# A chunked delta-rule recurrence with a gated output layer: the loads of SP put into the planned order, output stores of one batch row each, and the range flag computed inside the main path

## The chip, the cores and the metric

The kernel runs on one core of a Trainium2 chip. A core has five engines with a queue each: PE (TensorE, the matrix products), DVE (VectorE), ACT (ScalarE), POOL (GpSimd) and SP (SyncE, which here only issues DMAs). DMAs are issued from SP, ACT and POOL and move data between HBM and the on-chip SBUF. Every queue is worked off strictly in its order; an instruction that has to wait holds up all that stand behind it on its engine. The metric is the device time of one execution in microseconds. Three executions of the kernel before took 483.6 us in the median (479.5 to 491.18).

## The reference

For 4 batches and 8 heads a state of 40x40 is carried over 768 steps, read out before each update; the readings of all heads make a sequence of 320 channels, which goes through a causal convolution of 5 taps with a sigmoid (the gate), a product with `w_val`, and a product with `w_out`:

```python
for t in range(S):                                  # S = 768, state (4, 8, 40, 40) starts at 0
    y[:, :, t] = einsum('bhd,bhde->bhe', rt, state)
    Sa = einsum('bhde,bhe->bhd', state, at)
    state = state * wt[:, :, None, :] - einsum('bhd,bhe->bhde', Sa, bt) + einsum('bhd,bhe->bhde', vt, kt)
x = y.transpose(0, 2, 1, 3).reshape(B, S, 320)
gate = 1 / (1 + exp(-sum_k conv_w[k] * x_shifted[k]))   # 5 taps, causal
out = (gate * (x @ w_val)) @ w_out                      # float32, (4, 768, 320)
```

## The kernel before

The 768 steps are cut into 12 chunks of 64 (`C = 64`), and within a chunk the recurrence is written as matrix products. The 32 sequences (4 batches, 8 heads) lie as 16 pairs in two halves of the partitions. The work on a chunk `c` is made of these steps, which are the functions inside `fast_path`:

- `load`, `load2`, `load3`: SP loads of the chunk's inputs: `w` (the decays, 520 KB), `kb` (keys and b, 1 MB), `a` (512 KB), `vp` (320 KB), `vt` (1 MB) and `ra` (832 KB).
- `prep`: two scans on DVE over the decays (L409, L412), then the scaled `a`, `b` and `k` (L418, L420). On ACT, `far` and `out_of` (L416, L417) turn the decays into a measure, `wmx`, of whether any is outside the range for which the chunked form is exact; they overwrite the buffer of the decays, so the next decays can be loaded into it only after them. PE then makes a block product (`mb_`, L426), whose result ACT copies out in four pieces (`lst`, L430 and L433, and `mb`, L434).
- `ak` (PE L444, then DVE L446) and `turn` (transposes on PE L456, copied by ACT L458).
- `tri`: the inverse of 32x32 triangles for two chunks at once on DVE, a chain of short steps (L467, L488, L490, L494). `solve` puts the 64x64 inverse together from it (PE L513, L530, L538 with copies on ACT L534, L536 and L545).
- `chain`: the part that carries the state from chunk to chunk, in two halves (PE L561, L559, L570, L577, L587, L603, L601, L619), with copies on ACT and DVE between the products. Its output is `xe` (DVE L614).
- `moe`: `xd` moves `xe` into the channel layout `xt` by 12 small DMAs inside SBUF (8 for the first half of the heads, 4 for the second), issued from POOL (L664). The convolution starts on ACT (L669) and goes on with 12 steps on DVE (L673), the sigmoid is ACT L677, the first product PE L83 in two parts with DVE L679 and L682 behind them, the second product PE L106. ACT L686 copies the result out and ACT L688 stores it, two batches (160 KB) per DMA, so two stores a chunk.

`weigh` unpacks the weights at the start: five loads and 40 short DVE instructions (L45 to L52).

The order of all this is not written by hand: `Plan` holds each step with its engine, an assumed duration and what it reads and writes, lays out the steps by a list scheduler, and emits them in the order of the planned start. PE, ACT, DVE and POOL keep that order (`manual_schedule`, L732). SP is not in that list: its loads are in the plan, but their order on the queue is set by the framework's own scheduler afterwards. Which buffer of a ring a load goes to, and so what it waits for, is the same in both cases.

After the main path, `general_path` computes a flag from `wmx` (L747 to L753: a maximum on DVE, a transposition on PE, a second maximum and a comparison on DVE), every engine loads it into a register (L754) and branches (L755) past a step-by-step version of the whole computation, which runs only if a decay was out of range. The tiles of that path lie in memory that the main path used, so the flag's own tiles wait until the main path, its stores included, is done with it.

```python
    with tc.manual_schedule(engines={E.PE, E.Activation, E.DVE, E.Pool}):       # L732
        for t, e, d, n, fn in seq:
            fn()
```

## Time and profile before

| | |
|---|---|
| runs | 479.5, 483.6, 491.18 us; median 483.6 |
| profiled execution | 486.17 us, of which the span from the first to the last instruction is 484.3 |
| PE busy | 381.4 us (79%) |
| DVE busy | 361.0 us (75%) |
| ACT busy | 222.7 us (46%) |
| POOL busy | 80.6 us (17%) |
| PE clock granted, mean | 0.904 of full speed |
| chain that ended last | PE 52%, DVE 19%, DMA 11%, waiting for nothing that shows 8%, ACT 6% |

The share of an engine is a mean over stages with different limits, so it does not say what a stage is worth. The first 30 us are filled by loads (the DMA engines are busy at 0.9 and more, then fall off), from there to about 100 us DVE is nearly always busy, from 100 to 450 us PE and DVE share the load, and the last 35 us belong to the output layer of the last two chunks and to the end of the program. All times below are on the span's own clock, 0 being its first instruction.

### The profile page before, as it was taken

The numbers are of one execution on the slowest core, as the hardware profiler recorded it, in microseconds if no ns is written. First come the engines' busy times: TensorE is split into PE (matmuls) and PEld (weight loads), VectorE is DVE, ScalarE is ACT, GpSimd is POOL, SyncE is SP. The second block draws the span as 40 slices with busy tenths as digits, with TensorE's granted clock in tenths as the row PEclk, the third lists the DMA queues.
The fourth block names the chain that finished last, engine by engine and source line by source line (L and its number), as shares of the span: only waits on it lengthen the run. The fifth ranks groups of instructions, "written<-read, shape, count | busy, mean of one in ns | idle before, by whom it ended". The sixth has DMA issues, their size and how long they took to land.

```text
span 484.3 us, 19768 instructions
## 1 busy us (share of the span) xinstructions
PE 381.4 (79%) x8857; PEld 328.6 (68%) x8857; DVE 361.0 (75%) x743; ACT 222.7 (46%) x393; POOL 80.6 (17%) x193
## 2 busy tenths in 40 slices
PE   0337566979989899779699789899897996989850
PEld 0226456969868797668588577897777975879630
DVE  8747787997888999869869959999888863314510
ACT  3443446445576362664264475446754263133210
POOL 2000000040310311301300400405005031050500
PEclk9999575897999999989979979999998997988995
DMA  8943333045534537151646322565106052010110
GB/s 342 420 166 133 115 104 94 23 177 194 193 106 138 188 110 294 42 172 50 205 167 206 117 74 90 207 204 181 60 18 208 24 182 62 7 49 10 30 35 23
DMA packets 19048, 63.20 MB, mean 130 GB/s; under 512 B 4080, under 2 KB 8168, under 8 KB 15888
## 3 DMA queue, kind: packets, MB, share of 16 engines
q1 hardware_dynamic: 11232, 53.78, 31.4%
q0 software_dynamic: 4608, 4.19, 3.4%
q10 hardware_dynamic: 3120, 3.93, 2.5%
q8 instruction: 70, 1.15, 1.0%
q14 instruction: 18, 0.15, 0.1%
HBM read 53.77 MB, written 3.93 MB: 119 GB/s over the span
## 4 chain that ended last, share of the span: by engine, by line
PE 52%; DVE 19%; DMA 11%; issue 8%; ACT 6%; POOL 1%; SPq 1%; ACTq 0%; DVEq 0%; POOLq 0%
PE pm L83 8%; PE pc L587 6%; PE pc L601 5%; PE pp L456 5%; PE pp L444 4%; DMA xt<-xe 4%; DVE x L490 4%; DVE tm L488 3%; PE pm L106 3%; PE pc L577 3%; DMA w<-in_w 3%; PE pc L570 3%; PE pc L603 3%; DVE mu L589 2%; DVE ag L673 2%
## 5 line engine op out<-in xcount | busy, mean ns | idle before, releaser
L664 POOL DMA_DIRECT2D xt<-xe x144 | 72.9, 514 | 240.9 <-issue 84.3
L673 DVE SCALAR_TENSOR_TENSOR ag<-xt,wts,ag 128x256 f32<-128x256 f32 (+1 forms) x144 | 55.7, 433 | 42.4 <-ACT ag L669 42.1
L490 DVE TENSOR_TENSOR x<-x,tm 128x58 f32<-128x58 f32 (+9 forms) x164 | 52.1, 318 | 3.1
L488 DVE TENSOR_TENSOR tm<-x 128x58 f32<-128x58 f32 (+9 forms) x164 | 52.1, 318 | 3.0
L83 PE MATMUL pm<-xt,wts 128*128 128x128 f32 (+1 forms) x288 | 39.9, 304 | 11.3 <-issue 4.7
L587 PE MATMUL pc<-ra,vu 64*128 64x64 f32 x768 | 47.4, 273 | 0.0
L587 PEld LDWEIGHTS pc<-ra,vu 64*128 64x128 f32 x768 | 45.0, 188 | 2.1 <-issue 0.3
L83 PEld LDWEIGHTS pm<-xt,wts 128*128 128x128 f32 (+1 forms) x288 | 31.8, 188 | 16.3 <-issue 5.7
L601 PE MATMUL pc<-mu,kbt 128*64 128x104 f32 x768 | 39.8, 256 | 2.2 <-issue 2.2
L106 PE MATMUL pm<-wts,ag 128*128 128x320 f32 (+1 forms) x144 | 37.7, 456 | 1.6 <-DVE ag L682 1.6
L444 PE MATMUL pp<-at,kb 64*64 64x64 f32 x768 | 31.0, 248 | 10.0 <-ACT mb L434 8.2
L601 PEld LDWEIGHTS pc<-mu,kbt 128*64 128x64 f32 x768 | 34.8, 137 | 5.5 <-issue 2.3
L444 PEld LDWEIGHTS pp<-at,kb 64*64 64x64 f32 x768 | 29.4, 162 | 12.1 <-ACT mb L434 9.1
L456 PE MATMUL pp<-cst,kb 104*128 104x104 f32 x192 | 28.2, 303 | 11.6 <-DVE ak L446 9.9
L426 PE MATMUL pp<-at,kb 64*64 64x64 f32 x768 | 18.6, 259 | 21.4 <-DVE at L418 15.4
L561 PE MATMUL pc<-vp,ak 64*64 64x40 f32 x768 | 29.9, 252 | 3.8 <-issue 3.8
L456 PEld LDWEIGHTS pp<-cst,kb 104*128 104x128 f32 x192 | 22.9, 170 | 14.2 <-DVE ak L446 11.2
L426 PEld LDWEIGHTS pp<-at,kb 64*64 64x64 f32 x768 | 16.6, 170 | 22.8 <-DVE at L418 15.4
L409 DVE TENSOR_TENSOR_SCAN lam<-w,ind 104x1040 f32<-104x1040 f32 x11 | 25.4, 2308 | 9.0 <-DMA w<-in_w 9.0
L589 DVE TENSOR_TENSOR mu<-pc,cst 128x1024 f32<-128x1024 f32 x24 | 29.2, 1216 | 3.2 <-PE pc L587 3.1
L458 ACT COPY kbt<-pp 128x640 f32<-128x640 f32 x24 | 16.6, 691 | 31.6 <-PE pp L456 21.5
L559 PE MATMUL pc<-st,at 64*64 64x40 f32 x704 | 27.7, 247 | 3.9 <-issue 3.9
(104 smaller groups left out, 704.7 us busy)
## 6 DMA issues: line engine op xcount, KB each, us to landing
kb<-in_kb SPq DMA_DIRECT2D x12, 1024.0 KB
vu<-in_vt SPq DMA_DIRECT2D x12, 1024.0 KB
ra<-in_ra SPq DMA_DIRECT2D x12, 832.0 KB
at<-in_a SPq DMA_DIRECT2D x12, 512.0 KB
w<-in_w SPq DMA_DIRECT2D x11, 520.0 KB
vp<-in_vp SPq DMA_DIRECT2D x12, 320.0 KB
out<-xt ACTq DMA_DIRECT2D x24, 160.0 KB
xt<-xe POOLq DMA_DIRECT2D x72, 42.5 KB, 3.4
```

Of the source, the lines that this page charges most:

```text
L83: T.matmul(out=o, lhsT=wv[k][r, m * 128:min(m * 128 + 128, DM)], rhs=rhs, start=(k == 0), stop=(k == 2))
L106: nc.tensor.matmul(out=ps[:, j, 0:DM], lhsT=gv[r, q * C:q * C + 128], rhs=wo[k][r], start=(k == 0), stop=(k == 2))
L426: T.matmul(out=PP[rows(par ^ s, 64), s, q * C:q * C + C], lhsT=KB[kb][rk, 2 * q + s, 1], rhs=at[rk, 2 * q + s], start=True, stop=True)
L444: T.matmul(out=PP[r, s, q * C:q * C + C], lhsT=KB[kb][r, 2 * q + s, 0], rhs=AT[n][r, 2 * q + s], start=True, stop=True)
L456: T.transpose(out=PP[:, i // 4, i % 4 * 128:i % 4 * 128 + ER], in_=KB[kb][0:ER, 8 * x + i].rearrange("p b t -> p (b t)"), identity=ident[0 ...
L488: V.tensor_tensor(out=tv, in0=part(32 * (j + 1) + j, *b, (32, n), (0, j)), in1=part(32 * j, *b, (0, n), (1, j)), op=ALU.mult)
L490: V.tensor_tensor(out=x, in0=x, in1=tv, op=ALU.subtract)
L587: T.matmul(out=ps[:, s, i * C:i * C + C], lhsT=vu[r, 8 * hf + i].rearrange("p b t -> p (b t)"), rhs=ra[r, w, 0:C], start=True, stop=True)
L589: op(("ge", c, hf), "DVE", dve(1024), lambda: V.tensor_tensor(out=mu[:, :, 0:C].rearrange("p (i s) t -> p s i t", s=2), in0=ps.rearrange(" ...
L601: T.matmul(out=o, lhsT=KBT[k][:, y * D:y * D + C], rhs=mu[:, 2 * (4 * p + q4) + s], start=(not c and not q4), stop=(q4 == 3))
L664: G.dma_start(out=o, in_=x)
L673: op(("cv", c, j, k), "DVE", 90 + 1.05 * nn[k], lambda k=k, q=q, j=j: V.scalar_tensor_tensor(out=acc[:, q], in0=xt[:, q, j:j + C], scalar= ...
```

## The change

- SP joins the engines whose order is the plan's (`manual_schedule`).
- Each store is one batch row: four DMAs of 64 rows of 1280 bytes (80 KB) a chunk, all on ACT, except in the last chunk, where two of the four are on SP.
- The 12 small moves of `xd` of the last two chunks are issued from SP instead of POOL.
- The flag is computed by four steps of the plan (`beyond`) while the main path is still at work, in a tile that the main path's memory does not hold.
- The loop of the step-by-step path goes over 16 steps instead of 32, 48 times instead of 24, and its output product and store are cut to match; this path does not run here.

Since the plan is made anew with these durations, the order on all engines moves, not only on SP.

```diff
-CG = 32
+CG = 16
...
+    def beyond():
+
+        wm, w1 = new("wm", [ER, 1]), new("w1", [1, 1])
+        op("wm", "DVE", 200, lambda: V.tensor_reduce(out=wm, in_=wmx.rearrange("p c x -> p (c x)"), axis=AX.X, op=ALU.max), r=[("wmx", c) for c in range(nch)], w=["wm"])
+        op("wt", "PE", 350, lambda: T.transpose(out=PP[0:1, 0, 0:ER], in_=wm, identity=ident[0:ER, 0:ER]), r=["wm", "cst"], w=ppb[0:1])
+        op("w1", "DVE", 250, lambda: V.tensor_reduce(out=w1, in_=PP[0:1, 0, 0:ER], axis=AX.X, op=ALU.max), r=ppb[0:1], w=["w1"])
+        op("fl", "DVE", 150, lambda: V.tensor_scalar(out=fl, in0=w1, scalar1=0.0, scalar2=None, op0=ALU.is_gt), r=["w1"], w=["fl"])
...
         for hf in range(2):
+            late = c + 2 >= nch
+
             def xd(hf=hf):
                 for o, x in x_moves(xt, XE[i], C, hf):
-                    G.dma_start(out=o, in_=x)
-            op(("xd", c, hf), "POOL", (8, 4)[hf] * 600, xd, r=[("xe", i, hf), ("xe", i, "c"), "wts"], w=[("xt", i), ("os", i)], lat=2500)
+                    (nc.sync if late else G).dma_start(out=o, in_=x)
+            op(("xd", c, hf), "SP" if late else "POOL", (8, 4)[hf] * (400 if late else 600), xd, r=[("xe", i, hf), ("xe", i, "c"), "wts"], w=[("xt", i), ("os", i)], lat=2500)
...
-        for j in range(2):
-            op(("store", c, j), "ACT", 560, lambda j=j: A.dma_start(out=out[j * 2:(j + 1) * 2, c * C:c * C + C], in_=os[:, j * DM:j * DM + DM]), r=[("os", i)], lat=2500)
+        for b in range(B):
+            on, eng = ("SP", nc.sync) if c + 1 == nch and b % 2 else ("ACT", A)
+            op(("store", c, b), on, 560, lambda b=b, eng=eng: eng.dma_start(
+                out=out[b, c * C:c * C + C], in_=os[b % 2 * 64:b % 2 * 64 + 64, b // 2 * DM:b // 2 * DM + DM]), r=[("os", i)], lat=2000)
...
+        if c + 4 == nch:
+            beyond()
...
-    with tc.manual_schedule(engines={E.PE, E.Activation, E.DVE, E.Pool}):
+    with tc.manual_schedule(engines={E.PE, E.Activation, E.DVE, E.Pool, E.SP}):
...
-        wm = cp.tile([ER, 1], F32, name="wm")
-        V.tensor_reduce(out=wm, in_=wmx.rearrange("p c x -> p (c x)"), axis=AX.X, op=ALU.max)
-        ps = pp.tile([1, ER], F32, name="pg")
-        T.transpose(out=ps, in_=wm, identity=cst[0:ER, 0:ER])
-        w1 = cp.tile([1, 1], F32, name="w1")
-        V.tensor_reduce(out=w1, in_=ps, axis=AX.X, op=ALU.max)
-        fl = cp.tile([1, 1], I32, name="fl")
-        V.tensor_scalar(out=fl, in0=w1, scalar1=0.0, scalar2=None, op0=ALU.is_gt)
         flag = nc.values_load(fl, min_val=0, max_val=1)
```

Three places of the new order. The first is SP's queue at the start of the program, from its eighth load on (`ag` and `xt` take the packed weights here, `at` is `a`; the line numbers of the changed kernel are higher by one). Before:

```order
L330 DMA ag<-in_wts 128x646
L330 DMA at_73<-in_a 128x1024
L330 DMA at_74<-in_a 128x1024
L330 DMA xt<-in_wts 128x646
L330 DMA vp<-in_vp 128x640
L330 DMA vu_81<-in_vt 128x2048
L330 DMA ra_83<-in_ra 128x1664
L330 DMA vu_82<-in_vt 128x2048
L330 DMA ra_84<-in_ra 128x1664
L330 DMA w<-in_w 128x1040
```

Now:

```order
L331 DMA ag<-in_wts 128x646
L331 DMA w<-in_w 128x1040
L331 DMA at_74<-in_a 128x1024
L331 DMA at_75<-in_a 128x1024
L331 DMA xt<-in_wts 128x646
L331 DMA vp<-in_vp 128x640
```

The decays of chunk 2 have moved ahead of eight other loads, from the seventeenth place to the ninth.

The second is ACT's queue in the same stretch (`xe` holds the decays of chunk 1 here, so its two lines are `far` and `out_of` of that chunk; `lst` and `mb` are the copies of the block product of chunk 0, then of chunk 1). Before:

```order
L430 COPY lst<-pp 128x16x32
L433 COPY lst<-pp 32x16x32 x2
L434 COPY mb<-pp 128x512
L520 ACTIVATE n_92<-lst,cst 128x16x16 x2
L430 COPY lst<-pp 128x16x32
L433 COPY lst<-pp 32x16x32 x2
L434 COPY mb<-pp 128x512
L416 ACTIVATE xe_108<-xe_108,bias 104x16x64
L417 ACTIVATE xe_108,wmx<-xe_108,bias 104x16x64
```

Now:

```order
L431 COPY lst<-pp 128x16x32
L434 COPY lst<-pp 32x16x32
L417 ACTIVATE xe_109<-xe_109,bias 104x16x64
L434 COPY lst<-pp 32x16x32
L418 ACTIVATE xe_109,wmx<-xe_109,bias 104x16x64
L435 COPY mb<-pp 128x512
L529 ACTIVATE n_93<-lst,cst 128x16x16 x2
L431 COPY lst<-pp 128x16x32
L434 COPY lst<-pp 32x16x32 x2
L435 COPY mb<-pp 128x512
```

The two range instructions of chunk 1 stood behind the copies of both block products and now stand ahead of the last copies of the first.

The third is the end of the program on PE and ACT, from the last chunk's `chain` on (PE: L577 and L587 are its middle, L603 and L601 its end, L83 the first and L106 the second product of the output layer, first of chunk 10, then of chunk 11). PE before:

```order
L577 MATMUL pc_114<-cst,vu_82 128x104 x8
L587 MATMUL pc_113<-ra_84,vu_82 128x64 x16
L587 MATMUL pc_114<-ra_84,vu_82 128x64 x16
L603 MATMUL pc_113<-ra_84,zd 64x104 x16
L601 MATMUL pc_113<-mu_103,kbt_90 64x104 x16
L603 MATMUL pc_114<-ra_84,zd 64x104 x16
L601 MATMUL pc_114<-mu_104,kbt_90 64x104 x16
L83 MATMUL pm<-xt,wts 128x128 x4
L83 MATMUL pm<-xt,wz 128x128 x2
L83 MATMUL pm<-xt,wts 128x128 x4
L83 MATMUL pm<-xt,wz 128x128 x2
L83 MATMUL pm<-xt,wts 64x128 x4
```

PE now:

```order
L83 MATMUL pm<-xt,wts 128x128 x4
L83 MATMUL pm<-xt,wz 128x128 x2
L83 MATMUL pm<-xt,wts 128x128 x4
L83 MATMUL pm<-xt,wz 128x128 x2
L586 MATMUL pc_115<-cst,vu_83 128x104 x8
L596 MATMUL pc_114<-ra_85,vu_83 128x64 x16
L596 MATMUL pc_115<-ra_85,vu_83 128x64 x16
L612 MATMUL pc_114<-ra_85,zd 64x104 x16
L610 MATMUL pc_114<-mu_104,kbt_91 64x104 x16
L612 MATMUL pc_115<-ra_85,zd 64x104 x16
L610 MATMUL pc_115<-mu_105,kbt_91 64x104 x16
L83 MATMUL pm<-xt,wts 64x128 x4
```

ACT before, from the sigmoid of chunk 10 on:

```order
L677 ACTIVATE ag<-ag 128x640
L669 ACTIVATE ag<-xt,wts 128x256 x2
L669 ACTIVATE ag<-xt,wts 128x128
L686 COPY xt<-pm 128x640
L688 DMA out<-xt 2x64x320 x2
L677 ACTIVATE ag<-ag 128x640
L686 COPY xt<-pm 128x640
L688 DMA out<-xt 2x64x320 x2
L754 TENSOR_LOAD fl
```

ACT now:

```order
L688 ACTIVATE ag<-ag 128x640
L588 COPY mu_105<-pc_115 128x16x40
L697 COPY xt<-pm 128x640
L680 ACTIVATE ag<-xt,wts 128x256 x2
L680 ACTIVATE ag<-xt,wts 128x128
L700 DMA out<-xt 64x320 x4
L688 ACTIVATE ag<-ag 128x640
L697 COPY xt<-pm 128x640
L700 DMA out<-xt 64x320 x2
L761 TENSOR_LOAD fl
```

The larger part of chunk 10's first product has moved from behind the last `chain` into it, and the copy of chunk 10's result (L697, before L686) from behind the start of chunk 11's convolution to ahead of it.

## Rows read from the trace of the kernel before

**Rows 1.** The chain of waits, end of the program: start us, length us, what.

```profile
464.29 3.18 PE pm L106 x12
...
467.50 0.70 ACT xt L686
...
468.78 8.55 DMA out<-xt
...
477.65 0.18 DVE wm L747
...
478.57 0.14 DVE fl L753
```

**Rows 2.** Busy time by stretch (engines, granted PE clock, DMA share, GB/s).

```profile
473.70:477.00 3.30, 0.00 (x0) 0.00 (x0) 0.00 (x0) 0.00 (x0) 0.00 (x0) 0.50 0.13 48
5.00:16.00 11.00, 0.64 (x24) 0.65 (x28) 10.87 (x10) 2.39 (x3) 0.00 (x0) 1.00 1.01 412
```

**Rows 3.** Lines L754, L755, L870: count, ns min/median/max, first and last start.

```profile
L754 PEldq TENSOR_LOAD <-fl x1: 493/493/493, 478.9 to 478.9; - x1
...
L755 SPq EVENT_SEMAPHORE  x8: 17/17/17, 479.9 to 480.4; - x8
L755 SPq COMPARE_BRANCH  x1: 45/45/45, 479.4 to 479.4; - x1
...
L755 PEldq EVENT_SEMAPHORE  x1: 51/51/51, 483.3 to 483.3; - x1
...
L870 SPq EVENT_SEMAPHORE  x10: 17/28/2212, 480.8 to 484.3; - x10
```

**Rows 4.** Groups by form: count, busy us, mean ns, idle before and its releaser.

```profile
L409 DVE TENSOR_TENSOR_SCAN lam<-w,ind 104x1040 f32<-104x1040 f32 x11 | 25.4, 2308 | 9.0 <-DMA w<-in_w 9.0
...
L418 DVE TENSOR_TENSOR at<-at,lam 104x1024 f32<-104x1024 f32 x12 | 14.3, 1192 | 0.0
```

**Rows 5.** The chain of waits at the head, columns as in rows 1.

```profile
4.75 11.23 DMA at<-in_a
16.07 13.78 DMA w<-in_w
```

**Rows 6.** Timeline of the head: start, length, engine, line, what, idle before, releaser.

```profile
24.36 2.02 ACT L433 COPY lst<-pp 32x512 f32<-32x512 f32 x2
...
26.88 1.15 ACT L416 ACTIVATE xe<-xe,bias 104x1024 f32<-104x1024 f32 x1
...
27.04 3.68 PE L444 MATMUL pp<-at,kb 64*64 64x64 f32 x64 [3.79 <-ACT mb L434]
...
29.97 2.33 DVE L409 TENSOR_TENSOR_SCAN lam<-w,ind 104x1040 f32<-104x1040 f32 x1 [9.02 <-DMA w<-in_w]
...
36.39 1.22 DVE L446 TENSOR_TENSOR ak<-pp,cst 128x1024 f32<-128x1024 f32 x1
```

**Rows 7.** Issues of the stores; ACT's waits by line (total us, times, longest).

```profile
L688 ACTq DMA_DIRECT2D out<-xt x24: 521/527/1122, 144.2 to 468.8; - x24
...
ACT xx L534 <- PE pm L530: 19.7, 9, 4.9
```

**Rows 8.** Tile xt, 440 to 460 us: the small moves, and issue to landing.

```profile
L664 POOL DMA_DIRECT2D xt<-xe x12: 502/512/522, 449.3 to 454.8; - x12
...
DMA to landing us min/median/max: 1.6/1.7/1.8
```

**Rows 9.** The chain of waits: the first products of chunks 9 and 10.

```profile
405.27 5.85 PE pm L83 x24
...
449.67 3.04 PE pm L83 x24
```

**Rows 10.** Timeline of chunk 11's convolution, columns as in rows 6.

```profile
456.73 0.80 ACT L669 ACTIVATE ag<-xt,wts 128x256 f32<-128x256 f32 x2 [0.99 <-DMA xt<-xe]
...
461.21 0.74 ACT L677 ACTIVATE ag<-ag 128x640 f32<-128x640 f32 x1 [2.35 <-DVE ag L673]
```

**Rows 11.** Busy time by stretch, columns as in rows 2: chunk 9's first product.

```profile
405.20:411.20 6.00, 5.93 (x25) 4.80 (x26) 4.39 (x12) 2.17 (x5) 0.00 (x0) 0.50 0.01 5
```

More of the change, by code (lines that the diff above doesn't have):

```diff
@@ L96, in out_mms @@
             q = 8 * L if k == 2 else (4 * k + 2 * h) * L
-            nc.tensor.matmul(out=ps[r], lhsT=gv[rk, q:q + 64], rhs=wo[k][rk], start=(k == 0), stop=(k == 2))
+            nc.tensor.matmul(out=ps[h * 64:h * 64 + 2 * L], lhsT=gv[rk, q:q + 2 * L], rhs=wo[k][rk], start=(k == 0), stop=(k == 2))
 def out_mms2(nc, ps, gv, wo):
@@ L135, in moe_steps @@
     os_ = mo.tile([128, DM], F32, name="os", bufs=1)
-    A.copy(out=os_, in_=ps[:, 0:DM])
-    for b in range(B):
-        store(b, os_[b * L:b * L + L])
+    for h in (0, 64):
+        A.copy(out=os_[h:h + 2 * L], in_=ps[h:h + 2 * L, 0:DM])
+        for j in range(2):
+            store(h // 32 + j, os_[h + j * L:h + j * L + L])
 class Plan:
@@ L271, in act, with fast_path @@
     return 165 + 0.84 * n
-def fast_path(ctx, tc, ins, out, nch, cst, wts, wz, wmx):
+def fast_path(ctx, tc, ins, out, nch, cst, wts, wz, wmx, fl):
     nc = tc.nc
@@ L416, in prep @@
         op(("far", c), "ACT", act(1024) + 100, lambda: A.activation(out=wv, in_=wv, func=AF.Abs, bias=bias[:, 0:1]), r=["bias"], w=wk)
-        op(("out_of", c), "ACT", act(1024) + 290, lambda: A.activation(out=wv, in_=wv, func=AF.Relu, bias=bias[:, 1:2], accum_out=wmx[:, c]), r=["bias"], w=wk)
+        op(("out_of", c), "ACT", act(1024) + 290, lambda: A.activation(out=wv, in_=wv, func=AF.Relu, bias=bias[:, 1:2], accum_out=wmx[:, c]), r=["bias"], w=wk + [("wmx", c)])
         op(("at", c), "DVE", 65 + 1.05 * 1024, lambda: V.tensor_tensor(out=at[0:ER], in0=at[0:ER], in1=lam[:, :, 0:C], op=ALU.mult), r=[("lam", n)], w=[("at", n)])
@@ L731, in fast_path, with general_path @@
     seq = plan.order()
-    with tc.manual_schedule(engines={E.PE, E.Activation, E.DVE, E.Pool}):
+    with tc.manual_schedule(engines={E.PE, E.Activation, E.DVE, E.Pool, E.SP}):
         for t, e, d, n, fn in seq:
             fn()
-def general_path(tc, ins, out, nch, cst, wts, wz, wmx):
+def general_path(tc, ins, out, nch, cst, wts, wz, fl):
     nc = tc.nc
@@ L793, in general_path @@
                     V.tensor_tensor(out=s, in0=s, in1=t2, op=ALU.add)
[L794 removed]
+                V.tensor_copy(out=xe[:, :, 0:4], in_=xe[:, :, CG:CG + 4])
                 for par in range(2):
                     r = slice(par * 64, par * 64 + 40)
[L797 removed]
+                    V.tensor_copy(out=xe[r, :, 4:CG + 4], in_=py[r].rearrange("p t u -> p u t"))
                 moe_steps(nc, mo, pp, wts, wz, xe, xt, lambda b, o: nc.sync.dma_start(out=out[b, bass.ds(c * CG, CG)], in_=o))
@@ L807, in rwkv_kernel @@
         wmx = keep.tile([ER, nch, 1], F32, name="wmx")
+        fl = keep.tile([1, 1], I32, name="fl")
         with ExitStack() as ctx:
-            fast_path(ctx, tc, ins, out, nch, cst, wts, wz, wmx)
-        general_path(tc, ins, out, S // CG, cst, wts, wz, wmx)
+            fast_path(ctx, tc, ins, out, nch, cst, wts, wz, wmx, fl)
+        general_path(tc, ins, out, S // CG, cst, wts, wz, fl)
 def lay_out(r, k, v, w, a, b, moe_w_val, moe_conv_w, moe_w_out):
```

2 lines of the change are left out of this document (removed).

## The prediction

> **What bounds the kernel now.** The chain of waits comes first, read from its end. ACT's last copy is over at 468.20; after it nothing is computed but the flag. The second store of the last chunk is issued at 468.78 and lands at 477.33, the flag's steps take 1.1 us from 477.65 to 478.71, and the span ends at 484.3 [rows 1]: 16.1 us behind the last useful instruction. Busy time by stretch says why the landing is late: while the two stores are all that moves, the DMA engines are busy at 0.13, two of sixteen, and move 48 GB/s; the first loads, spread over 128 partitions, keep all busy (1.01) at 412 GB/s [rows 2]. The lines of the branch show what follows the flag: PE loads its register at 478.9 and is past the branch at 483.3, 4.4 us later, and 1.0 us after that the span ends. SP goes from its branch at 479.4 over eight semaphore resets (0.07 apart) to its final waits at 480.8 [rows 3]. None of this is work, and all of it stands in a row, because the flag waited for the stores and the branch for the flag.
>
> At the other end of the program the groups by form show that, of all scans of the decays, those of L409 lost 9.0 us to a load [rows 4]. The chain at the head shows which load: that of chunk 2's decays, issued at 16.07 and landed at 29.85 [rows 5]. DVE stood still for 9.02 us ahead of 29.97, that is from 20.95 on [rows 6]. Between the two ends PE and DVE share the time and no load is waited for at this scale, so there only the new order can cost or give something.
>
> **The end of the program.** From 468.20 on, ACT issues its two stores of the last chunk and SP its two at the same time; an issue takes 0.53 [rows 7], so the last ones start at 468.78, as before. The landing of a store of one batch is in no row. The near end: the small moves inside SBUF land 1.6 to 1.8 us after their issue when nothing else is in flight [rows 8]. The far end: 8.55 us, as now [rows 1]. I take 2.0. A batch row has 64 outer rows, like the loads' 128 partitions and unlike the two batches of the present store, so I expect all sixteen engines, and then 80 KB at 412 GB/s are 0.2 us on top of 1.8. That is 470.8. SP then needs the 1.4 us from its branch to its final waits and about 0.4 for six more of those at 0.07 [rows 3], and the program 1.0 to end: 473.6. PE isn't later: it waits for no store any more, its last product ends at 467.47 [rows 1], and 4.4 us for register and branch make 471.9, under the store's shadow. Against 484.3 that is **-10.7**. The flag itself leaves the end. Ends of this term: -12 (landing after 1.6, part of the resets done ahead of it), and -4.2 with the far landing (477.33 + 1.8 + 1.0 = 480.1).
>
> The Trainium skill, DMA: Bandwidth & Descriptors, section "Why a DMA increments its semaphore by 16 and not by 1", says that a DMA runs on the largest number of engines up to 16 that divides the slowest dimension above 1 of both sides: two for the store of two batches, which the trace bears out (0.13 of the engines), and sixteen for one batch, which no row here shows. The same page's "Rules for kernel authors" speaks against the change: merge small transfers, since under 64 KB overhead is most of them. With its fit of 2.0 us plus 436 GB/s, a store of 160 KB would be an estimated 2.4 us and one of 80 KB 2.2, so splitting would give 0.2 and the sum would keep the rest only if the stores were not slow now. The trace disagrees, with 8.55 us.
>
> **The head.** Chunk 2's decays become SP's ninth load. Their buffer is free once chunk 0's two range instructions are through, which head ACT's queue in both orders. The load that is ninth now, of the same size, lands at 15.98 [rows 5]. So these land at about 16, before DVE wants them, and the 9.02 us go. What is late next: DVE's queue now holds, between 20.95 and the first triangle, the scan, a second one of the same length (2.31), a scaling (1.19) and a few short steps that I put at 1 us, some 6.8 to 27.7 [rows 4]. The triangle needs ACT's copies of chunk 1's block product, which ended at 26.38 [rows 6]. But the two range instructions of chunk 1, 1.15 each, which stood behind them, now stand ahead of chunk 0's last copies, so all copies behind are 2.3 later: 28.7 for the triangle, and the PE product, begun at 27.04, ends at 27.04 + 2.3 + 3.68 = 33.0. DVE's masking, next in its queue, starts then instead of at 36.39. New idle: 1.0 ahead of the triangle, and, its transposition (1.2, as the masking) done at 29.9, about 3.1 between it and the masking. Of 9.02 remain 4.9 on DVE, 3.4 on PE's side. But by the first inverse the new queue has three times the weight unpacking behind it, 21 of the 40 steps instead of 7, and the first inverse is what the chain of chunk 0 waits for. So I take **-2**; ends: 0 (all spent on moved work) and -9.
>
> **The last two chunks.** Before, chunk 10's first product (3.04 and a smaller rest) ran wholly behind the last chain [rows 9]; now the larger part is ahead of its middle. That shortens what comes behind and lengthens the chain by up to 3.04. Chunk 11's layer cannot use the gain: its convolution needs the moved `xe`, the last of which arrives at 456.73 in the present trace [rows 10], 7.1 after the chain's end at 449.67, and ACT's sigmoid at 461.21 waits for that convolution. ACT's new order puts chunk 10's copy ahead of the convolution, where ACT waits for the moves anyway. So the time from the chain's end to the end of ACT's last copy (468.20 - 449.67 = 18.5) stays, but PE now has little to do in the first 7.1 us of it. What such a gap costs is seen in chunk 9: after its wait for the moves the first product took 5.85 at a granted clock of 0.50 (1.2 instead of 2.4 GHz), not 3.04 [rows 9, 11]. Here the smaller rest and the 3.18 of the last product would follow, which at half the clock and double the time is up to about 4 more. With 0 to 3.0 for the chain and 0 to 4 for the clock I take **+2**, near the lower end, since the chain has gaps to fill.
>
> **Costed at nothing.** Two more store issues on ACT in each of eleven chunks: next on ACT come copies that wait for PE anyway (19.7 us in nine waits, 2.2 each, against 1.1) [rows 7]. Without that cover it is 22 x 0.53 = 11.6. The flag's four steps, 1.1 us [rows 1], stand beside DVE's wait for chunk 10's moves; bare they are 1.1. The 24 moves on SP: an SP issue is in no row that shows its length; ACT's of 0.53 and POOL's of 0.51 are the nearest [rows 7, 8], so I take the moves to be issued no later. Their landing from SP is in no row; 1 us either way is the bound, worth as much at the end. Behind them on SP stand only the flag's register and two stores. The general path doesn't run.
>
> **Sum.** -10.7 - 2 + 2 = -10.7 against the profiled execution's 486.2 (484.3 of span and 1.9 around it): 475.5. The median of the runs is 2.6 lower, so 472.9, said as **473**.
>
> **Rivals.** (a) *The head's gain holds*: DVE is nearly always busy from 30 to 100 us, so that idle time taken out there may carry through; against it, ACT's new order makes PE wait. With -9 for -2 and nothing lost at the end: 464. (b) *The end of chunk 11 eats more*: clock and chain at their bounds, +7, and nothing from the head: 480. (c) *A store of one batch lands no sooner* (on few engines, or because four share them): -4.2 for -10.7 is 479.5; the loads' row speaks against it. (d) *Slower*: ACT's added issues are not covered. The place is behind each chunk's output copy, ahead of the copies that `solve` and `chain` wait for; it decides as soon as ACT reaches those copies later than PE has their input, that is when the 2.2 us of mean wait shrink below 1.1. Then +11.6 stand against -10.7, and with (b)'s +7 it is 491. (e) *The loads move but nothing waits less*: the decays' place is seen in the order, so only the 2 us of the head are at stake: 475.
>
> **Numbers.** About 2% is what a measurement of this kernel can tell from no change, that is 473.9 or less for faster and 493.3 or more for slower. The forecast has 0.56 (467 to 479; some three fifths of it under 473.9), (a) 0.16, (b) 0.13, (c) 0.05, (d) 0.06, (e) 0.04. That makes 0.52 faster, 0.45 within 2%, 0.03 slower. The range runs from (a) to short of (d): 463 to 484.
>
> **What would show it.** Right: the last landing about 2 us after its issue, a DMA share near 1 for a moment, and less than 6 us from ACT's last copy to the end; no wait of L410 for a load; DVE's first masking near 33. Wrong: more than 8 us behind the last copy (first step); a wait of DVE for a load anywhere, or the first chain's output no earlier than before (second); a time from the last chain to the last copy far from 18.5 (third); ACT's copies behind the stores waited for by PE (rival d).

## The result, and the profile after

The changed kernel takes 468.47 us in the median of 4 runs (466.9 to 470.34), the kernel before 483.99 beside it; the ratio is 0.9711 (0.9631 to 0.9791), so it is faster. The forecast was 473, with a range from 463 to 484. The profiled execution took 468.85, with a span of 467.1, against 486.17 and 484.3. Some executions of a kernel come out a few per cent slower than its others: the ratios here and below leave out those more than 1.5% above the fastest, the medians do not.

The number came out near, but not by the sum that gave it. The span falls into four stretches; the bounds are the end of chunk 0's and of chunk 11's chain (the last `xe` of each, DVE) and the end of ACT's last copy (the prediction's 18.5 from the last chain to the last copy begins 0.7 earlier, at PE's end of that chain):

| profiled execution, us | before | changed | difference | forecast |
|---|---|---|---|---|
| start to the end of chunk 0's chain | 104.8 | 113.2 | +8.4 | -2 for all up to the last chains |
| from there to the end of chunk 11's chain | 345.6 | 325.6 | -20.0 | not in the sum |
| last chain to ACT's last copy | 17.8 | 21.7 | +3.9 | +2 |
| last copy to the end | 16.1 | 6.6 | -9.5 | -10.7 |

**The end.** The chain of waits of the changed kernel, its last part (start, length, what), now stops at ACT's last copy; no wait for a store or a flag stands in it [rows 1]:

```profile
453.49 1.05 PE pm L83 x12
...
454.90 4.85 PE pm L106 x12
...
459.82 0.69 ACT xt L697
```

The line of the branch, L762 (count, ns, first and last start) [rows 3]:

```profile
L762 SPq EVENT_SEMAPHORE  x8: 17/17/17, 464.8 to 465.4; - x8
...
L762 PEldq COMPARE_BRANCH  x1: 375/375/375, 455.6 to 455.6; - x1
...
L762 PEldq EVENT_SEMAPHORE  x1: 51/51/51, 459.8 to 459.8; - x1
L762 SPq COMPARE_BRANCH  x1: 45/45/45, 462.0 to 462.0; - x1
```

PE's queue takes the branch at 455.6, while its last products still run, and is through at 459.8, under ACT's last copy. Busy time by stretch shows the four row stores (columns as in rows 2; the DMA share is the last but one):

```profile
461.70:463.20 1.50, 0.00 (x0) 0.00 (x0) 0.00 (x0) 0.00 (x0) 0.00 (x0) 0.71 0.82 224
```

The four move at 0.82 of the engines and 224 GB/s, where two stores of two batches had 0.13 and 48. What is new at the end is on SP: it branches at 462.0 and does its first reset only at 464.8, 2.8 us later, where it took 0.5 before (479.4 to 479.9) [rows 3].

**The head.** Groups by form: the scan L410 (L409 before) waits 0.1 instead of 9.0 [rows 4]:

```profile
L413 DVE TENSOR_TENSOR_SCAN y<-w,ind 104x1040 f32<-104x1040 f32 x11 | 25.4, 2312 | 0.0
L410 DVE TENSOR_TENSOR_SCAN lam<-w,ind 104x1040 f32<-104x1040 f32 x11 | 25.3, 2302 | 0.1
```

The timeline shows what came in its place [rows 6]:

```profile
22.03 2.31 DVE L410 TENSOR_TENSOR_SCAN lam<-w,ind 104x1040 f32<-104x1040 f32 x1
22.74 1.15 ACT L418 ACTIVATE xe<-xe,bias 104x1024 f32<-104x1024 f32 x1
...
27.74 2.02 ACT L434 COPY lst<-pp 32x512 f32<-32x512 f32 x2
...
29.80 1.25 DVE L476 STREAM_TRANSPOSE x<-lst 128x1024 f32<-128x1024 f32 x1 [1.77 <-ACT lst L434]
...
30.43 3.68 PE L445 MATMUL pp<-at,kb 64*64 64x64 f32 x64 [3.81 <-ACT mb L435]
...
34.21 1.22 DVE L447 TENSOR_TENSOR ak<-pp,cst 128x1024 f32<-128x1024 f32 x1 [3.17 <-PE pp L445]
```

ACT's copies are 3.4 us later than before (27.74 for 24.36), and DVE waits 1.77 and 3.17 for them and for PE; its first masking is at 34.21, 2.2 earlier than before. Yet chunk 0's chain ends 8.4 later. Busy time over the stretch ahead of it, first of the changed kernel, then of the experiment `e9_head` (below), which has the old order there:

```profile
78.00:111.00 33.00, 30.59 (x594) 28.52 (x593) 22.57 (x58) 11.92 (x25) 3.92 (x13) 0.56 0.05 12
```

```profile
78.00:100.00 22.00, 21.17 (x565) 19.59 (x556) 21.86 (x61) 10.12 (x21) 3.99 (x8) 0.88 0.23 71
```

PE does about as many products in both (594 and 565) and is busy nearly all the time in both, but at a granted clock of 0.56 it needs 30.6 us for them instead of 21.2. The low clock lasts for 29.3 us of the first stretch and for 5.3 of the second; half of the difference is 12.0, and the stretches differ by 11.0. So by this estimate, which takes each us at half clock as half a us lost, what the new order loses ahead of chunk 0's end is the clock of the last stretch. No run has the new order there at full clock.

**The middle.** The same view from the end of chunk 0's chain to the end of chunk 11's, before, then changed:

```profile
104.80:450.40 345.60, 308.59 (x7398) 265.69 (x7399) 272.58 (x558) 172.28 (x318) 66.74 (x151) 0.93 0.38 127
```

```profile
113.20:438.80 325.60, 296.04 (x7428) 255.78 (x7428) 271.55 (x558) 169.59 (x317) 59.96 (x136) 0.97 0.42 135
```

DVE is busy for the same 272 us. PE is busy for 12.6 less with as many products (some records are missing): its mean granted clock is 0.97, not 0.93. Added up over the stretch, the trace grants 1.2 instead of 2.4 GHz for 47.8 us before and for 17.1 now.

**The last chunks.** The moves of chunk 11, tile xt, and then the granted clock behind them [rows 8, 11]:

```profile
L675 SPq DMA_DIRECT2D xt<-xe x12: 637/717/768, 436.5 to 445.4; - x12
```

```profile
445.00:460.00 15.00, 11.51 (x48) 7.53 (x48) 5.38 (x14) 2.23 (x5) 0.00 (x0) 0.66 0.13 33
```

An issue on SP takes 0.72 us, on POOL it took 0.51, and the last product takes 4.85 instead of 3.18.

### The profile page after: what moved, and what is told of

It is laid out like the page before. It is cut to its first block, busy times and chain, and to the rows that moved or that the text cites. A ratio compares the mean times of both kernels' runs of the same rounds, so it can differ in the third digit from the quotient of the medians.

```text
span 467.1 us, 19760 instructions
## 1 busy us (share of the span) xinstructions
PE 378.6 (81%) x8857; PEld 327.4 (70%) x8857; DVE 361.1 (77%) x743; ACT 220.3 (47%) x393; POOL 68.7 (15%) x169
## 4 chain that ended last, share of the span: by engine, by line
PE 51%; DVE 22%; ACT 11%; issue 8%; DMA 4%; SPq 3%; ACTq 1%; POOL 0%; DVEq 0%
PE pc L596 6%; PE pp L445 6%; PE pm L106 6%; PE pc L610 6%; DVE ag L684 6%; PE pp L457 5%; DMA xt<-xe 3%; PE pm L83 3%; SPq L675 3%; PE pc L612 3%; ACT lst L434 3%; PE pp L427 3%; PE pc L570 2%; PE pm L522 2%; PE pc L586 2%
## 5 line engine op out<-in xcount | busy, mean ns | idle before, releaser
L675 POOL DMA_DIRECT2D xt<-xe x120 | 61.1, 515 | 187.2 <-issue 82.1
L596 PE MATMUL pc<-ra,vu 64*128 64x64 f32 x768 | 49.6, 282 | 1.7 <-ACT mu L588 1.7
L596 PEld LDWEIGHTS pc<-ra,vu 64*128 64x128 f32 x768 | 46.9, 196 | 4.2 <-ACT mu L588 1.9
L83 PE MATMUL pm<-xt,wts 128*128 128x128 f32 (+1 forms) x288 | 38.8, 297 | 9.9 <-DVE ag L690 3.3
L610 PE MATMUL pc<-mu,kbt 128*64 128x104 f32 x768 | 41.9, 265 | 0.2 <-DVE mu L598 0.2
L83 PEld LDWEIGHTS pm<-xt,wts 128*128 128x128 f32 (+1 forms) x288 | 31.0, 183 | 14.5 <-issue 6.3
L427 PE MATMUL pp<-at,kb 64*64 64x64 f32 x768 | 18.5, 260 | 27.6 <-DVE at L419 16.3
L106 PE MATMUL pm<-wts,ag 128*128 128x320 f32 (+1 forms) x144 | 39.5, 470 | 0.8 <-DVE ag L693 0.8
L610 PEld LDWEIGHTS pc<-mu,kbt 128*64 128x64 f32 x768 | 37.0, 143 | 4.0 <-issue 0.7
L427 PEld LDWEIGHTS pp<-at,kb 64*64 64x64 f32 x768 | 16.5, 169 | 29.0 <-DVE at L419 16.3
L106 PEld LDWEIGHTS pm<-wts,ag 128*128 128x128 f32 (+1 forms) x144 | 21.6, 193 | 13.9 <-issue 6.5
L570 PE MATMUL pc<-vp,ak 64*64 64x40 f32 x768 | 26.4, 237 | 5.6 <-issue 5.6
L421 DVE TENSOR_TENSOR kb<-kb,y 104x1024 f32<-104x1024 f32 x24 | 28.9, 1209 | 1.3 <-DMA kb<-in_kb 1.2
```

The lines of the kernel that those rows point to most:

```text
L83: T.matmul(out=o, lhsT=wv[k][r, m * 128:min(m * 128 + 128, DM)], rhs=rhs, start=(k == 0), stop=(k == 2))
L106: nc.tensor.matmul(out=ps[:, j, 0:DM], lhsT=gv[r, q * C:q * C + 128], rhs=wo[k][r], start=(k == 0), stop=(k == 2))
L427: T.matmul(out=PP[rows(par ^ s, 64), s, q * C:q * C + C], lhsT=KB[kb][rk, 2 * q + s, 1], rhs=at[rk, 2 * q + s], start=True, stop=True)
L570: T.matmul(out=o, lhsT=AKM[k][rows(par, 64), m], rhs=VP[rows(par, 64), m], start=True, stop=not c)
L596: T.matmul(out=ps[:, s, i * C:i * C + C], lhsT=vu[r, 8 * hf + i].rearrange("p b t -> p (b t)"), rhs=ra[r, w, 0:C], start=True, stop=True)
L610: T.matmul(out=o, lhsT=KBT[k][:, y * D:y * D + C], rhs=mu[:, 2 * (4 * p + q4) + s], start=(not c and not q4), stop=(q4 == 3))
```

## The experiments

Two theories at first. A: the parts of the change, SP's order first, bring the last chain forward. B (later C): the new order of PE, DVE and ACT does, by way of PE's clock. The table has all runs: the median, the ratio to the kernel before, and, from the one trace of each, the four stretches, with the time at half clock inside the second (low) and that stretch less half of it. The clock of the first stretch is not in the table, because its record begins late, between 8 and 86 us by kernel, and the views show 1.00 ahead of it (see `e12_early`).

| kernel | median | ratio (95%) | chunk 0 | to chunk 11 | low | less low/2 | to last copy | to end |
|---|---|---|---|---|---|---|---|---|
| before | 484.0 | 1 | 104.8 | 345.6 | 47.8 | 321.7 | 17.8 | 16.1 |
| changed | 468.5 | 0.971 (0.963 to 0.979) | 113.2 | 325.6 | 17.1 | 317.1 | 21.7 | 6.6 |
| e1_sp | 484.1 | – | 98.2 | 347.6 | 51.2 | 322.0 | 17.8 | 16.2 |
| e2_rows | 475.3 | 0.976 (0.964 to 0.988) | 104.9 | 331.1 | 23.9 | 319.2 | 17.8 | 10.2 |
| e3_flag | 486.9 | – | 107.1 | 347.1 | 44.4 | 324.9 | 17.8 | 11.5 |
| e4_three | 462.6 | 0.944 (0.935 to 0.954) | 99.1 | 342.7 | 44.4 | 320.5 | 17.8 | 6.6 |
| e5_no_sp | 476.1 | 0.981 (0.973 to 0.990) | 114.3 | 331.7 | 34.1 | 314.6 | 22.1 | 6.5 |
| e6_pool | 464.0 | 0.962 (0.954 to 0.969) | 110.8 | 325.6 | 17.1 | 317.1 | 20.0 | 4.9 |
| e7_order | 479.5 | 0.990 (0.982 to 0.998) | 111.6 | 330.3 | 23.9 | 318.4 | 19.7 | 16.3 |
| e8_warm | 472.1 | 0.973 (0.966 to 0.981) | 109.8 | 332.2 | 30.7 | 316.8 | 21.7 | 6.6 |
| e9_head | 456.0 | 0.926 (0.918 to 0.935) | 100.5 | 327.3 | 23.9 | 315.4 | 19.5 | 4.9 |
| e10_both | 446.9 | 0.919 (0.912 to 0.925) | 102.2 | 324.8 | 20.5 | 314.6 | 19.6 | 5.0 |
| e11_busy | 474.4 | 0.974 (0.968 to 0.979) | 107.7 | 346.0 | 61.4 | 315.3 | 18.6 | 4.9 |
| e12_early | 476.7 | 0.986 (0.971 to 1.002) | 111.1 | 338.7 | 37.5 | 319.9 | 18.5 | 5.0 |

The kernel before took 484 to 489 in the median beside these runs, so the ratios compare better than the medians. By their intervals `e4_three`, `e9_head` and `e10_both` are faster than the changed kernel and `e7_order` is slower; those of the others that have one overlap with its own, and there only the traces speak. Each trace is one execution: those of `e4_three`, `e10_both` and `e11_busy` took 5, 6 and 5 us more than their medians, that of `e2_rows` 9 us less.

**SP's order alone**, `e1_sp`:

```diff
-    with tc.manual_schedule(engines={E.PE, E.Activation, E.DVE, E.Pool}):
+    with tc.manual_schedule(engines={E.PE, E.Activation, E.DVE, E.Pool, E.SP}):
```

> The kernel before with SP's loads in the plan's order and nothing else changed; the order of PE, DVE, ACT and POOL is that of before. Both theories: DVE's wait of 9.02 us for chunk 2's decays goes, and with ACT's copies where they were (they end at 26.38) DVE's first masking starts at about 31 instead of 36.39. Theory A (the 11.6 us by which the changed kernel ends its last chain earlier come from its parts, SP's order first): at least 5 us of it carry through to the end of the last chain, 444 or earlier instead of 449.7, and the kernel takes 476 to 479. Theory B (they come from the new order of the work on PE, DVE and ACT): under 3 us carry through, because the idle time moves to the next wait, and the kernel takes 481 to 484.

Measured: 484.1 where the kernel before had 489.0 (479.4 to 486.9, and 484.4 upwards), which is no clear difference. The trace has the first masking at 30.64 and chunk 0's chain 6.6 earlier; the last chain ends at 445.8, so 4.6 are left. By the last chain this lies between the two theories: of the 9.0 us of waiting, 6.6 show at the end of chunk 0's chain and 4.6 at the end of chunk 11's. The kernel's time is not theory A's (476 to 479).

**Row stores alone**, `e2_rows`:

```diff
+            def store(j=j):
+                for b in (2 * j, 2 * j + 1):
+                    (nc.sync if c + 1 == nch and b % 2 else A).dma_start(
+                        out=out[b, c * C:c * C + C], in_=os[b % 2 * 64:b % 2 * 64 + 64, j * DM:j * DM + DM])
-            op(("store", c, j), "ACT", 560, lambda j=j: A.dma_start(out=out[j * 2:(j + 1) * 2, c * C:c * C + C], in_=os[:, j * DM:j * DM + DM]), r=[("os", i)], lat=2500)
+            op(("store", c, j), "ACT", 560, store, r=[("os", i)], lat=2500)
```

> The kernel before, each store step issuing two stores of one batch row where it issued one of two batches; the order of the steps is that of before, the flag still waits for the stores. Both theories: the last store lands about 2 us after its issue, as in the changed kernel, instead of 8.55, so the span ends about 6 us earlier, 478 in all. Theory A expects 1 to 3 us more in the body, since the stores' buffer comes free earlier in each chunk (475 to 477); theory B none, and up to 2 us against it for 22 more issues on ACT (478 to 480). If a row store lands as late as the store of two batches, 484.

Measured: 475.3 (465.9 to 484.5), in theory A's range, but too widely spread to rule out theory B's. The view of tile xt for the last four stores (times from issue to landing, min, median, max):

```profile
DMA to landing us min/median/max: 2.1/2.3/2.4
```

2.3 us where a store of two batches took 8.55 [rows 1], and 5.9 off the end. The rest is in the middle, where the low clock happened to be 23.9; less half of that, the stretch is 2.5 shorter than before, so 22 more issues on ACT cost nothing that shows. With the old order this middle is as short as that of the new order at the same low time (331.1, and 330.3 in `e7_order`, both with 23.9), so the clock weighs more there than the order of the work.

**Early flag alone**, `e3_flag` (and the same four steps taken out of `general_path`):

```diff
             fn()
+            if n == ("xd", nch - 2, 1):
+                wm, w1 = new("wm", [ER, 1]), new("w1", [1, 1])
+                V.tensor_reduce(out=wm, in_=wmx.rearrange("p c x -> p (c x)"), axis=AX.X, op=ALU.max)
+                T.transpose(out=PP[0:1, 0, 0:ER], in_=wm, identity=ident[0:ER, 0:ER])
+                V.tensor_reduce(out=w1, in_=PP[0:1, 0, 0:ER], axis=AX.X, op=ALU.max)
+                V.tensor_scalar(out=fl, in0=w1, scalar1=0.0, scalar2=None, op0=ALU.is_gt)
```

> The kernel before with the flag computed early, its four instructions placed behind the issue of chunk 10's moves, everything else in the order and form of before. Both theories: the branch on PE is through before the stores land, the span ends about 1.5 to 3 us after the last landing at 477.3 instead of 7, so 4 to 5.5 us less: 479 to 480. If what follows the branch needed the stores in any case, 484.

Measured: 486.9 (476.8 to 490.1), so the forecast time was missed and no difference is shown in the runs. In the trace the end is 4.6 shorter, as expected. All ahead of it is 3.8 longer, but chunk 10's chain, ahead of the first instruction that differs, was already 5.7 late, so this is the scatter of one execution.

**The three parts on the old order of steps**, `e4_three` (the three edits together):

> The three parts together (SP in the plan's order, row stores, early flag) on the order of steps of before; the moves of the last two chunks stay on POOL. Both theories: the end of the program gives 9.5 to 10.7, as in the changed kernel. Theory A: the body gives another 8 to 11, so 463 to 467, and it is as fast as the changed kernel (468.5) or faster by the 3.9 us that the changed kernel loses between its last chain and its last copy. Theory B: the body gives under 3, so 471 to 474, slower than the changed kernel.

Measured: 462.6, faster than the changed kernel by ratio (0.944 and 0.971, intervals apart). The end gives 9.5. So the parts are worth more than the change as it was made, as theory A said, and ahead of the last chain's end its trace is 8.6 shorter (5.7 at the head, 2.9 in the middle), within theory A's 8 to 11. 1.7 of the 2.9 are half of 3.4 us less at half clock, which may be the scatter of one execution.

**The change without SP's order**, `e5_no_sp` (the first diff reversed on the changed kernel):

> The changed kernel with SP left out of the engines whose order is the plan's, nothing else changed. Theory A (SP's order is worth in the changed kernel what it is worth alone, where it brought the end of chunk 0's chain from 103.3 to 96.7): DVE waits for chunk 2's decays again, for 5 us or more, and the kernel takes 473 to 476 instead of 468.5. Rival: in the new order ACT's range instructions and the weight steps hold the head up anyway, so the loads have time to arrive in any order: 468 to 470.

Measured: 476.1. DVE waits 6.90 for chunk 2's decays again, but chunk 0's chain is only 1.1 later; 6.1 are in the middle, with 17 us more at half clock. Half of those 17 us is more than the 6.1, so the middle's loss may be scatter, and the intervals of the two ratios overlap. DVE's wait comes back as theory A said, but what shows of it at chunk 0's end is 1.1 us and not 6.6: there the trace agrees with the rival.

**The late moves on POOL**, `e6_pool`:

```diff
-                    (nc.sync if late else G).dma_start(out=o, in_=x)
+                    G.dma_start(out=o, in_=x)
```

> The changed kernel with the 24 small moves of the last two chunks issued from POOL again, at the same place in the order. In the changed kernel the moves of chunk 11 are issued 0.81 us apart on SP, 0.51 on POOL before. Theory: the last of them lands 2.3 us earlier, ACT's convolution starts so much earlier, and the gap in which PE's granted clock falls to 0.50 gets shorter; from the last chain's end to the end of ACT's last copy 18.5 to 20.1 us instead of 22.4, the kernel 464.5 to 466.5. Rival: the last chunk is held by something else (the convolution on DVE, the clock), so 468 to 469.

Measured: 464.0, half a us under the theory's range, though the ratio's interval overlaps with the changed kernel's. The moves are 0.51 apart again, and 1.7 go between chain and copy, less than the 2.3 to 3.9 expected: PE's last product takes 5.74 here, not 4.85. Another 1.7 go at the end:

```profile
L762 SPq EVENT_SEMAPHORE  x8: 17/17/17, 458.4 to 459.7; - x8
...
L762 SPq COMPARE_BRANCH  x1: 45/45/45, 457.9 to 457.9; - x1
```

SP starts its resets 0.5 us behind its branch, not 2.8. Why it stood in the changed kernel was not tried. The trace has a load of instructions, 8 KB, that starts at 463.1, behind SP's branch at 462.0; in `e6_pool` none starts between the branch and the first reset. The Trainium skill, Runtime: NRT & Kernel Launch, section "Instruction fetch mechanics", says that a taken branch to code outside what an engine has loaded waits for a fetch; SP's queue was 24 issues longer there, which would fit.

**The new order without the parts at the end**, `e7_order` (on the changed kernel: stores of two batches, flag behind the main path, moves on POOL; the edit is cut to the stores):

```diff
-                out=out[b, c * C:c * C + C], in_=os[b % 2 * 64:b % 2 * 64 + 64, b // 2 * DM:b // 2 * DM + DM]), r=[("os", i)], lat=2000)
+                out=out[b:b + 2, c * C:c * C + C], in_=os[:, b // 2 * DM:b // 2 * DM + DM]), r=[("os", i)], lat=2000)
```

> The changed kernel's order of steps on all engines, SP's included, but with the stores of two batches, the flag computed behind the main path and all small moves on POOL, as before. Against the run with SP's order alone (profiled at 481.5) it differs by the order of PE, DVE and ACT only. Theory C (the new order is what brings the chain of chunk 11 from 449.7 to 438.1, because PE is granted half its clock for 17 us between 120 and 440 instead of 41): the last chain ends at 437 to 440, the kernel takes 474 to 477. Rival A (the order costs its 15 us at the head and the row stores gave the rest back): the last chain ends at 444 or later, the kernel takes 481 or more.

Measured: 479.5, last chain at 441.9: between the two. The middle is short without the row stores (330.3, with 23.9 low). It loses 13.4 to `e1_sp` at the head and wins 17.3 behind it.

**Extra products in the last gap**, `e8_warm`:

```diff
+            if n == ("out", nch - 2):
+                for k in range(NWARM):
+                    T.matmul(out=PC[k % 2][:, 0, 0:320], lhsT=cst[:, 0:128], rhs=wts[:, 0:320], start=True, stop=True)
```

> The changed kernel with 12 extra products (128x320, results unused, about 0.5 us each) on PE between chunk 10's last product and chunk 11's first, where PE has nothing to do while the small moves are under way. Theory C (an idle PE lowers its granted clock, and the last chunk pays for it): the granted clock stays at 1.00 through chunk 11's products, its second product takes 3.1 us instead of 4.85, and the kernel is 1.5 to 3 us faster than the changed one, 465.5 to 467. Rival: the clock falls for another reason, and the second product still takes 4.85; 468.5, or more if the extra products delay it.

Measured: 472.1, by ratio no different from the changed kernel (0.973 and 0.971); the rival's. The clock stayed at 1.00 while the extra products ran, and was gone for the product that mattered:

```profile
445.50:452.30 6.80, 6.80 (x28) 4.83 (x27) 1.56 (x4) 2.00 (x4) 0.00 (x0) 1.00 0.13 38
458.10:463.00 4.90, 4.83 (x12) 2.71 (x12) 0.00 (x0) 0.00 (x0) 0.00 (x0) 0.65 0.03 7
```

**The old order at the head, the new one behind it**, `e9_head` (on `e6_pool`; HEAD is the list of 293 steps):

```diff
+HEAD = [
...
-    seq = plan.order()
+    step = {x[3]: x for x in plan.order()}
+    ends = set(HEAD) | set(TAIL)
+    seq = [step[n] for n in HEAD + [n for n in step if n not in ends] + TAIL]
```

> The changed kernel with the late moves on POOL (the run that took 464.0), its first 293 steps, up to the end of chunk 0's chain, put in the order that they had before, all others in the new order. Both orders have done the same work at that point but for four short DVE steps, so what the two orders are worth ahead of it and behind it can be added. Theory D (the new order loses 12 to 15 us up to the end of chunk 0's chain and wins 14 to 20 behind it, where PE's granted clock is low for 14 to 32 us instead of 38 to 44): chunk 0's chain ends at 98 to 99 instead of 111 to 113, the stretch from there to the end of chunk 11's chain stays at 326 to 332, and the kernel takes 450 to 456. Rival (what is lost at the head is given back behind it in any order, since the later work only waits for something that comes at its own time): the last chain ends at 434 to 438 again and the kernel takes 461 to 465.

Measured: 456.0, the upper end of theory D's range. The stretches add: 100.5 and 327.3. (Its "38 to 44" of low clock for the old order leaves out `e2_rows`, with 20.5 behind 120 us.) What the new order loses at the head is not given back by itself.

**The old order at both ends**, `e10_both` (the same, with a list for TAIL):

> As the run with the old order at the head, with the steps from chunk 10's last output on (chunk 10's and 11's output layer, chunk 11's chain) in the order of before as well; only the middle has the new order. Theory: the time from the last chain's end to the end of ACT's last copy is 17.8 as in every kernel with the old order there, instead of 20.0, and the clock stays at 1.00 through the last products, but chunk 10's first product stands behind the last chain again: 0 to 2 us less than the run with the old head alone. Rival: moving chunk 10's product into the chain was worth what it cost; same time or up to 2 us more.

Measured: 446.9, the lowest median here, 9.1 under that of `e9_head` where 0 to 2 were expected; the intervals of the two ratios overlap. In the trace the last stretch is 19.6, not 17.8, with the last product at 4.85 again, so the theory failed; the two profiled executions (453.35 and 453.99) are alike, and what makes the other five of this kernel 2 to 8 us shorter, no trace shows.

**Extra products at the head**, `e11_busy`:

```diff
+IDLE = {('kr', 1, 1): 2, ('mb_', 2): 10, ('kr', 2, 1): 2, ('rb', 0): 3}
+            for k in range(IDLE.get(n, 0)):
+                T.matmul(out=PC[k % 2][:, 0, 0:320], lhsT=ZD[:, 0:128], rhs=ZD[:, 0:320], start=True, stop=True)
```

> The changed kernel with the late moves on POOL and 17 extra products of zeros (128x320, results unused) on PE at four places between 47 and 78 us where PE waits for others; all else in the new order. Theory C (the new order is late at chunk 0's chain because PE's granted clock is 0.50 from 77 to 107, after stretches in which PE had little to do): the granted clock stays at 1.00 over most of 66 to 107, chunk 0's chain ends at 102 to 106 instead of 110 to 113, and the kernel takes 457 to 461. Rival (the order itself is late there, with DVE's weight steps and the copies on ACT ahead of the first inverse): chunk 0's chain ends at 109 or later, the kernel takes 463 to 467.

Measured: 474.4, 10 us slower than without them by the medians (the intervals of the two ratios touch), and both sides missed it. They held the clock at 0.99 from 50 to 65, where it was 0.50 without them. From 81.0 to 101.5 PE, busy for 20.50 of 20.50 us, was granted half of it all the same:

```profile
50.00:65.00 15.00, 11.99 (x178) 9.06 (x172) 10.80 (x27) 7.54 (x9) 0.00 (x0) 0.99 0.29 106
74.20:81.00 6.80, 4.30 (x197) 3.58 (x197) 5.23 (x17) 3.68 (x9) 0.21 (x4) 1.00 0.02 5
81.00:101.50 20.50, 20.50 (x286) 19.13 (x283) 12.54 (x32) 6.32 (x12) 0.00 (x0) 0.50 0.01 2
```

In the middle the low time is 61.4. That work alone keeps the clock up, as this trial of theory C had it, falls. That idle time brings it down is not refuted: in the 6.8 us ahead of the fall at 81.0 PE was busy for 4.30.

Chunk 0's chain ends 3.1 earlier than in `e6_pool`, so the loss is all behind it.

**Extra products that move nothing**, `e12_early`:

```diff
+            if n == ("pad", len(pads) - 1):
+                for k in range(NEARLY):
+                    T.matmul(out=PP[:, k % 2, 0:320], lhsT=ZD[:, 0:128], rhs=ZD[:, 0:320], start=True, stop=True)
```

> The changed kernel with the late moves on POOL and 20 extra products of zeros (128x320, results unused) on PE from about 4 to 14 us, where PE has nothing to do before its first product at 16.3; the order is the same and nothing is moved by them. In the run with 17 extra products between 47 and 78 us, PE was granted half its clock for 54.6 us behind 120 us instead of 13.7, and the kernel took 474.4 instead of 464.0. Theory E (work that PE does early is taken out of its clock later): the granted clock is low for 40 us or more behind 120 us again, and the kernel takes 471 to 476. Rival F (those 17 products did it by where they stood, by what they moved): the time is that without extra products, 463 to 467, with 14 to 28 us of low clock behind 120 us.

Measured: 476.7, 12.7 more than without them, 0.7 above theory E's range and far above rival F's; on another chip, but the ratios (0.986 and 0.962) have intervals that are just apart. The low time behind 120 is 35.3, between the two. Chunk 0's chain ends at 111.1 as in `e6_pool` (110.8), so nothing that matters was moved, and the loss is in the middle (338.7 for 325.6). The clock is on record as low from 22 on:

```profile
3.00:16.00 13.00, 12.69 (x38) 8.71 (x39) 12.49 (x13) 2.39 (x3) 0.26 (x1) 1.00 0.98 386
16.00:35.00 19.00, 7.66 (x196) 6.63 (x194) 14.35 (x14) 13.31 (x16) 1.15 (x7) 0.66 0.78 306
35.00:60.00 25.00, 14.73 (x236) 13.07 (x238) 20.43 (x57) 9.69 (x13) 0.00 (x0) 0.50 0.41 138
```

But that is not what the extra products changed. In `e6_pool` the record of the clock begins at 45.7, and the view shows 1.00 for all time ahead of it, while PE is busy there for as long:

```profile
16.00:35.00 19.00, 7.65 (x192) 7.08 (x192) 14.05 (x14) 13.35 (x16) 1.15 (x7) 1.00 0.77 307
```

Its products say what the clock was: eight equal ones take 1.65 us at 35.5 and 0.93 at 46.5, where the record has 1.00:

```profile
16.30 1.99 PE L427 MATMUL pp<-at,kb 64*64 64x64 f32 x64 [16.30 <-DVE at L419]
...
35.51 1.65 PE L457 MATMUL pp<-cst,kb 104*128 104x104 f32 x8 [1.38 <-DVE ak L447]
...
46.47 0.93 PE L457 MATMUL pp<-cst,kb 104*128 104x104 f32 x8 [1.40 <-DVE ak L447]
```

So PE ran at half clock up to about 45 us without the extra products too, and with them the first product that counts, at 16.84, took 1.16 instead of 1.99. A stretch or a mean clock that takes in time ahead of the first record, such as the 0.904 for the whole kernel before (record from 46.6 on; the same eight products take 1.65 at 37.7), is too high.

## Why the prediction was right, and where it was wrong

**The end: right, 1.2 us too much.** -10.7 forecast, -9.5 measured, and its two causes were measured apart, 5.9 for the stores (`e2_rows`) and 4.6 for the flag (`e3_flag`), and together at 9.5 (`e4_three`). A row store lands after 2.3 us, 2.0 was said, and by 0.82 of the engines. The Trainium skill, DMA: Bandwidth & Descriptors, section "Why a DMA increments its semaphore by 16 and not by 1", gives sixteen engines for such a store; 0.82 of the sixteen, 13 in the mean, agrees. Its advice to merge small transfers, weighed in the prediction, would have kept the 8.55. The end is 6.6, between the "less than 6" that was to show it right and the "more than 8" that was to show it wrong. The step that was mis-sized is SP's: 1.4 from its branch to the final waits was taken from before, and 3.4 went to its last reset alone (462.0 to 465.4), 1.7 of it with the moves on SP.

**The head: the step failed.** It was right on the wait (9.0 to 0.1), on what would be late next (1.77 and 3.17 of new waits, 1.0 and 3.1 forecast) and on the masking (34.2, 33.0 forecast; the copies came 3.4 later, 2.3 said). It then took 3.4 us on PE's side as kept, less some for the weights, and said -2. Chunk 0's chain ended at +8.4, one of the prediction's own signs of being wrong ("no earlier than before"). SP's order is worth -6.6 there in the old order of the other engines (`e1_sp`) and -1.1 in the new one (`e5_no_sp`); the new order costs 9.5 without SP's and 12 to 15 with it. What the step left out is the clock in the stretch just ahead of that chain's end: 0.56, worth an estimated 12 of the 12.7 us to `e9_head`. In every trace with the new order at the head there is a low stretch of 20 us or more that ends between 101 and 108; in those of the old order the last low stretch ahead of that chain's end is over by 91. That this clock and not the order alone makes the chain late is read from these traces; `e11_busy`, which was to show it, didn't keep the clock. Why the clock is low there stays open.

**The middle: missing from the sum.** That "there only the new order can cost or give something" was said of it, and nothing put; it gave 20.0, the largest term of all. The columns on the low clock size it: each us at half clock costs about half a us, and without that the old order takes 319 to 325 and the new one 315 to 320. So of the 20.0 an estimated 15.4 are clock (30.7 us less of it, halved) and 4.6 the order of the work; PE's busy time, 12.6 shorter, says a little less for the clock. The low time is not the order's alone: 17 to 34 in seven traces whose middle has the new order and no extra products in it or ahead of it, 24 to 51 in five with the old. So a part of the 15.4 is the luck of single executions.

**The last chunks: right in kind, +3.9 for +2** (22.4 by the prediction's own bounds, for 18.5). The lower clock was foreseen (4.85 for 3.18), though `e10_both` has it with the old order there too. That the moves from SP are "issued no later" was wrong: 0.72 an issue, not 0.51; `e6_pool` gives 3.4 of the span back in these two stretches; its median is 4.5 lower, which its ratio alone doesn't show. The first product of chunk 10 in the chain cost nothing that shows.

**Costed at nothing:** the store issues and the flag's steps, rightly as far as the traces of `e2_rows` and `e4_three` show. The moves on SP, costed at nothing too, are in the last chunks.

So 473 came near 468.5 by luck: two misses of opposite sign stood against each other, the head 10.4 us worse than said and the middle, which had no term, 20.0 better. None of the rivals was this case.

## What to carry to other kernels

What stands behind the last useful instruction is a chain like any other: look at how many DMA engines the last store uses and at what a final decision waits for; here 9.5 of 16.1 us went. When a planner lays out the whole program anew, the local edit is the smaller part: compare the two orders stretch by stretch, at points where both have done the same work, and keep the better piece of each; 456 us came from that at the head, and 447 with the old end as well, with no part added. Where PE is the bound, read its granted clock in that stretch first, and hold it against the length of equal products: the record can begin late.

## What the runs showed of the hardware

Twenty products of zeros on PE between 3.3 and 16.9 us, where it had nothing to do, made the kernel 12.7 us slower in the median (464.0 to 476.7, on another chip; ratios 0.962 and 0.986). The head was no later for it (111.1 and 110.8); behind it the clock was granted at half for 37.5 us instead of 17.1, in one trace of each. And PE that was busy for 20.50 of 20.50 us from 81.0 to 101.5 was granted 0.50 throughout (`e11_busy`). The Trainium skill, TensorE: Matmul & The Clock Gate, section "HAM oscillation — how this bites in real kernels", tells to leave PE no idle gaps, so that it keeps its clock. In this kernel that held where the extra products stood (0.99 from 50 to 65 us in `e11_busy`, for 0.50) and not later, where `e11_busy` and `e12_early` lost more than they had gained. What sets the clock here stays open: the traces show when it is low, not why.

Row stores, which run on 0.82 of the engines in the changed kernel, land after 2.3 us (`e2_rows`); a store of two batches, on 0.13 of them, took 8.55 in the kernel before. An issue of the same small move takes 0.72 us on SP and 0.51 on POOL.
